# Hashed attention and a squared-ReLU layer: a table that shifts the order's priorities, and one more head in float32

## The chip, the cores and the metric

The kernel runs on one core of one Trainium2 chip. The metric is the device time of one execution in microseconds (us); lower is better. The core has a matrix engine (TensorE, PE; its weight loads are shown apart as PEld), a vector engine (VectorE, DVE), a scalar engine (ScalarE, ACT), a general engine (GpSimd, POOL) and a queue engine for DMAs (SyncE, SP). Each runs its own instructions strictly in the order in which the program lists them, and waits at an instruction until what it needs is there.

## The reference

Attention over 4 batches, 8 heads, 768 positions and 64 values per position, in which a query sees only keys of its own hash bucket (6 bits, the signs of six projections):

```
q_bits = (q @ proj > 0);  k_bits = (k @ proj > 0)
mask   = q_bucket[:, None] == k_bucket[None, :]
scores = where(mask, 0.125 * q @ k.T, -1e9)
attn   = exp(scores - max(scores));  attn = attn / (sum(attn) + 1e-9)
x      = attn @ v                       # reshaped to 3072 tokens x 512
h      = x @ w_in                       # 512 -> 2048
out    = (s * max(h, 0)**2 + b) @ w_out # 2048 -> 512
```

## The kernel before

A *slot* is 256 queries of one head of one batch: 96 slots, three to a head, in the order of the batches. For a slot PE multiplies queries and keys into three PSUM banks (L569 or L571, "lead"), DVE takes the row maximum (L577) and finishes it over a transpose that PE makes (L588, L592, then L590 and L599), PE adds the maximum's row and the low parts to the scores ("closing" matmuls, L609 or L611), ACT takes the exponentials (L616, three pieces of 512 columns), and PE multiplies them with the values (L639, or L641 and L642). The product goes through a division (L681 to L684) and a store to memory (`xd`, L686).

There are two forms. In a *plain* head (batch 0) the exponentials stay float32 and PE multiplies them in one float32 matmul (L639), with the sum of exponentials as ones beside the values. In the other heads each piece is split into a high part (ACT, L634) and a low part (POOL, L635), which PE multiplies in two matmuls (L641, L642), and the sum comes from DVE (L661) and two short matmuls (L669). Four heads of batch 0 have exact scores in float32 (buffers `eqa`, `eqb`); the others have split scores, whose hash rows are moved into place by DMAs on SP's queue (L458 to L461, L489 to L492; the last of them is `aq<-nat`). Exponentials of plain slots go around nine buffers, three to a slot.

The weights come as 64-bit words and are decoded to float32 high and low parts by ACT, DVE and POOL (L363 to L375, 32 times) during the first slots. From slot 23 on the expert layer can run: for 256 tokens PE multiplies with `w_in` (L718), ACT squares (L723 to L725), POOL makes the low part (L726), and PE multiplies with `w_out` (L735).

What sets the order: the program first records every step with its engine, a cost, what it reads and writes, and a priority `pr` (10 per slot, 1e5 and more for expert matmuls, 1e4 for the rest of the expert layer). `Plan.order` (L73) then plays the steps through: at each turn the engine that can start first takes, of its ready steps, the one of the lowest priority (L112 to L117). The result is written out engine by engine. So a priority does not move a step past what it depends on, but decides which ready step goes first; expert matmuls fill what is left.

Of the kernel before, what the change touches and what calls it, by code (L numbers as in the profile page):

```python
# [10 lines left out]
F32 = mybir.dt.float32  # L11
# [20 lines left out]
class Plan:  # L32
# [39 lines left out]

    def order(self):  # L73
        n = len(self.steps)
        left = [len(s[5]) for s in self.steps]
        users = [[] for _ in range(n)]
        for i, s in enumerate(self.steps):
            for d in s[5]:
                users[d].append(i)
        ready, other = [0.0] * n, [-9.0] * n  # L80
        free = {}
        moved = 0.0
        used = {}
        holder, todo, until, again, soon = {}, dict(self.size), {}, {}, []

        def clear(i, e):
            b = self.half.get(i)
            t = max([t for (n, o), t in used.items() if n == b and o != e], default=-9.0)
            if i in self.lock and self.lock[i][0] not in holder:
                t = max(t, again.get(self.lock[i][0], -9.0))  # L90
            return t

        def may(i):
            if i not in self.lock:
                return True
            b, g = self.lock[i]
            return holder.get(b, g) == g and (b != 4 or g in soon or g in holder.values() or all(self.steps[i][3] + BEHIND <= self.steps[j][3] for j in soon))
        open_ = {}
        for i in range(n):
            if not left[i]:  # L100
                open_.setdefault(self.steps[i][0], []).append(i)
        out = []
        while len(out) < n:
            best = None
            for e, every in open_.items():
                lst = [i for i in every if may(i)]
                if lst:
                    t = max(free.get(e, 0.0), min(max(ready[i], clear(i, e)) for i in lst))
                    if best is None or t < best[0]:
                        best = (t, e)  # L110
            t, e = best
            rank = lambda i: (self.steps[i][3], i)  # L112
            at = {i: max(ready[i], clear(i, e)) for i in open_[e] if may(i)}
            safe = [i for i in at if at[i] <= t and max(other[i], clear(i, e)) + self.soft.get(i, CHAIN) <= t] if e == PE else []
            i = min(safe, key=rank) if safe else min((i for i in at if at[i] <= t), key=rank)
            if not safe:
                i = min((j for j in at if at[j] <= t + LOOK.get(e, 0.0) * self.steps[i][1] and rank(j) <= rank(i)), key=rank)  # L117
            open_[e].remove(i)
            eng, cost, fn, pr, lag, deps = self.steps[i]
            start = max(free.get(e, 0.0), at[i])  # L120
            free[e] = start + cost
            end = start + cost + HOP[e]
            if e == SP:
                moved = max(moved, start + cost) + lag
                end += moved - start - cost
            else:
                end += lag
            out.append((start, i))
            if i in self.soon:
                soon.append(self.soon[i])  # L130
            if i in self.lock:
                b, g = self.lock[i]
                holder[b] = g
                todo[g] -= 1
                until[b] = max(until.get(b, -9.0), end)
                if not todo[g]:
                    again[b] = until[b]
                    if g in soon:
                        soon.remove(g)
                    del holder[b]  # L140
            if i in self.half:
                used[self.half[i], e] = end
            for u in users[i]:
                ready[u] = max(ready[u], end - (SAME[e] if self.steps[u][0] == e else 0.0))
                if self.steps[u][0] != e:
                    other[u] = max(other[u], end)
                left[u] -= 1
                if not left[u]:
                    open_.setdefault(self.steps[u][0], []).append(u)
        self.length = max(free.values())  # L150
        self.start = {i: t for t, i in out}
        return [i for _, i in sorted(out)]
# [5 lines left out]
CHAIN = 0.05  # L158
OFF = 0.4
BEHIND = 8.0  # L160
TURN = 1
LOOK = {DVE: 0.5, ACT: 0.0, POOL: 0.0}


# [1 line left out]
def lsh_attention_moe(ctx: ExitStack, tc, q, k, v, proj, w_in, w_out, s, b, out):  # L166
    nc = tc.nc
    B, H, S, D = q.shape
    DM, DF = w_in.shape
    P = 128  # L170
# [16 lines left out]
    wk = ctx.enter_context(tc.tile_pool(name="wk", bufs=1))  # L187
# [4 lines left out]
    bank = ps.tile([P, 8, 512], F32, name="bank")  # L192
# [5 lines left out]
    def tile_(name, shape, dt=F32):  # L198
        return const.tile(shape, dt, name=name)
# [44 lines left out]
    MX = tile_("mx", [P, CH])  # L244
# [11 lines left out]
    osb = tile_("osb", [P, 2, DM])  # L256
    misc = tile_("misc", [P, 8])
    thr, big, s_sb, b_sb, qk_sb = [misc[:, x:x + 1] for x in range(5)]


    ident = tile_("ident", [P, P])
    make_identity(nc, ident)

    for _ in range(10):
        nc.tensor.matmul(bank[:, 7, 0:P], ident, ident, start=True, stop=True)


    for x in SETS:
# [9 lines left out]
    for i in range(2):  # L278
        rows = slice(i * 64, (i + 1) * 64)
        for r in range(2):  # L280
            c = at[i] + r * NBITS
# [22 lines left out]
    for ks in KS:  # L304
        nc.vector.tensor_copy(ks[0:NR, 1], ones[0:NR].broadcast_to([NR, S]))
    nc.vector.tensor_copy(oner, ones.broadcast_to([P, P]))
    nc.vector.memset(MX, 0.0)
    for y in range(2):
        nc.vector.tensor_copy(zhl[:, y], MX)
    for x, y in ((s, s_sb), (b, b_sb)):  # L310
# [4 lines left out]
    visits, slots = [], []  # L315
# [22 lines left out]
            dec.append((w_out_w[f * P:(f + 1) * P, :], ("wo", f)))  # L338
    ND = len(dec)

    def decode(u, pr):
        src, key = dec[u]
        box = {}

        def new():
            box["t"] = wk.tile([P, 512, 2], I32, tag=f"w{u}", name=f"raw{u}")

        def swap():
            wt[key] = wk.tile([P, 2, 512], F32R, tag=f"w{u}", name=f"w{u}")

        def raw():
            return box["t"]
        rk, wk_ = [("raw", u)], [key + (0,), key + (1,)]
        g, gk = osb[:, u % 2, :], ("os", u % 2)
        gi = g.bitcast(I32)

        held = []
        if u >= NB:
            z = SETS[(u - NB) // 3]
            held = ([("vs", z, 0), ("vs", z, 1)], AK(z), KK(z))[(u - NB) % 3]  # L360
        plan.add(None, 0.0, new, [], rk + held, pr - 5)
        plan.add(ACT, 0.1, lambda: nc.scalar.dma_start(raw(), src.rearrange("p (n t) -> p n t", t=2)), KK("a") if u < PACE else [], rk + [("pace", u % PACE)], pr - 5, 5.0)
        act(512, lambda: nc.scalar.activation(g, raw()[:, :, 1].bitcast(F32), AF.Copy, scale=float(2.0**-112)), rk + [("pace", u % PACE)], [gk], pr, 0.06)  # L363
        act(512, lambda: nc.scalar.activation(raw()[:, :, 0], raw()[:, :, 0].bitcast(U32), AF.Copy, scale=float(2.0**-29)), rk, rk, pr, 0.06)
        dve(256, lambda: nc.vector.tensor_scalar(raw()[:, :, 1], gi, -2**31, None, ALU.bitwise_and), [gk], rk, pr, 0.6)
        dve(512, lambda: nc.vector.scalar_tensor_tensor(gi, gi, 3, raw()[:, :, 1], ALU.logical_shift_left, ALU.bitwise_or), rk, [gk], pr, 0.92)
        pool(512, lambda: nc.gpsimd.tensor_tensor(gi, gi, raw()[:, :, 0], ALU.add), rk, [gk], pr)  # L367
        plan.add(None, 0.0, swap, [], rk + wk_, pr)
        act(512, lambda: nc.scalar.copy(wt[key][:, 0], g), [gk], [key + (0,)], pr)
        if key[0] == "wo":  # L370
            if key[1] == 0:
                pool(512, lambda: nc.gpsimd.tensor_copy(bcs, g), [gk], ["bcs"], pr + 5)
            else:
                pool(512, lambda: nc.gpsimd.tensor_tensor(bcs, bcs, g, ALU.add), [gk], ["bcs"], pr + 5)
        pool(512, lambda: nc.gpsimd.tensor_tensor(wt[key][:, 1], g, f32(wt[key][:, 0]), ALU.subtract), [gk, key + (0,)], [key + (1,)], pr)  # L375
# [17 lines left out]
    def KK(x, r=(0, 1, 2, 3, 4)):  # L393
        return [("ks", x, i) for i in r]
# [107 lines left out]
    def prep_values(w, pr):  # L502
        bb, h = visits[w]["bb"], visits[w]["h"]
        x = visits[w]["x"]
        vk = [("vs", x, 0), ("vs", x, 1)]
        vd = v[bb, h].rearrange("(p t) d -> p t d", t=NT)
        if not bb:
            if x not in SETS:
                def new():
                    EV[x] = wk.tile([P, NT, 2, D], F32, tag=f"vs{x}", name=f"vs{w}")  # L510
# [22 lines left out]
        mean(bb, h, pr)  # L533

    def plain(i):
        return not slots[i][0]

    def et(z):
        return E[z] if z < NE else HL[z - NE]
# [15 lines left out]
    def scores(i, pr):  # L555

        bb, h, c, w = slots[i]
        x, y = visits[w]["x"], i % 2
# [5 lines left out]
        for p in range(NP_):  # L564
# [5 lines left out]
                        continue  # L570
                    nc.tensor.matmul(o, ks[0:HR + NR, 0, kt], aq[0:HR + NR, cs], start=m == 0, stop=m == 1, skip_group_check=True)  # L571
            pe(mmc(CH, 8 if exact else 2), lead, AK(x) + KK(x) if exact else AK(x, g=CG[c])  + KK(x, (0, 2, 4)), [("b", pb[p])], pr, True)
        turn = slots[i][0] >= TURN
        t, tk, nm, nk = MX, "mx", nmt[:, turn], ("nm", turn)

        sc = bank[:, b0:b0 + NP_].rearrange("p b (m n) -> p n b m", n=CH)
# [189 lines left out]
    for i in range(NSL):  # L766
        pr = 10.0 * i
        bb, h, c, w = slots[i]
# [46 lines left out]
MP = 1e4  # L815
PP = 0


# [1 line left out]
_INS = ['q', 'k', 'v', 'proj', 'moe_w_in', 'moe_w_out', 'moe_s', 'moe_b']  # L820
_OUTS = [((3072, 512), 'float32')]
# [21 lines left out]
```

## Time and profile before

| | us |
|---|---|
| median of 3 runs (1036.47, 1041.07, 1041.07) | 1041.07 |
| the profiled execution | 1038.18 |
| its span, first to last instruction | 1036.4 |
| PE busy | 999.8 (96%) |
| DVE, ACT, POOL busy | 685.2, 673.6, 654.5 |

Busy times are of the span. PE and the others work side by side; only the time in which PE does not work can be gained without taking work from it. A PE record is drawn from its start to a modelled end and overlaps the next one. A float32 matmul is two records.

### The profile page before, as it was taken

The page shows a single profiled execution, that of the slowest core. Times are in us where ns is not written, and L with a number is a line of the kernel's source. Part 1 is how long each engine was busy: PE and PEld are TensorE (multiplying, and loading weights), DVE is VectorE, ACT ScalarE, POOL GpSimd, SP SyncE. Part 2 cuts the span into 40 slices and gives each one's busy share as a digit, 9 for nine tenths or more (in the row PEclk, how much of TensorE's full clock was granted, in tenths as well). Part 3 has the DMA queues.
Part 4 walks back from the last instruction along what each step waited for, and adds up shares of the span by engine and source line. Part 5 has one row for each costly group of instructions (what it writes and reads, how often), then busy time and mean ns, then how long its engine had stood idle before and what let it go on. Part 6 is the DMA issues. An engine that isn't in the chain of part 4 may idle for free.

```text
span 1036.4 us, 18211 instructions
## 1 busy us (share of the span) xinstructions
PE 999.8 (96%) x6662; PEld 898.0 (87%) x6662; DVE 685.2 (66%) x893; ACT 673.6 (65%) x1325; POOL 654.5 (63%) x596
## 2 busy tenths in 40 slices
PE   8989889889999999999999999999999999999998
PEld 6867767769899999999999988999999999899997
DVE  5778787876787787778787778877787876100000
ACT  4767776677676777777777767776777677333322
POOL 2566775697777776777777667767767776312221
PEclk9999999999999999999999999999999999999999
DMA  7565764522422332333432332332432220201000
GB/s 180 145 171 137 195 180 124 151 57 58 111 71 73 99 94 58 108 89 78 108 91 62 93 99 58 88 105 66 109 99 68 73 66 11 82 1 61 31 22 20
DMA packets 93681, 93.07 MB, mean 90 GB/s; under 512 B 62744, under 2 KB 66328, under 8 KB 93592
## 3 DMA queue, kind: packets, MB, share of 16 engines
q1 hardware_dynamic: 88392, 74.87, 27.3%
q10 hardware_dynamic: 5200, 17.05, 5.6%
q8 instruction: 52, 0.85, 0.3%
q14 instruction: 37, 0.30, 0.1%
HBM read 48.24 MB, written 18.87 MB: 65 GB/s over the span
## 4 chain that ended last, share of the span: by engine, by line
PE 86%; POOL 4%; DMA 3%; DVE 2%; ACT 2%; issue 2%; SPq 0%; DVEq 0%; ACTq 0%; POOLq 0%
PE bank L718 26%; PE bank L735 25%; PE bank L571 5%; PE bank L611 5%; PE bank L642 5%; PE bank L641 5%; PE bank L639 4%; PE bank L569 2%; PE bank L669 2%; PE bank L451 2%; DMA aq<-nat 1%; POOL hl L635 1%; POOL osb L367 1%; DMA xd<-xsb 1%; PE bank L592 1%
## 5 line engine op out<-in xcount | busy, mean ns | idle before, releaser
L635 POOL TENSOR_TENSOR hl<-et,hl 128x512 fp32r<-128x512 f32 x216 | 279.6, 1321 | 119.9 <-ACT hl L634 100.6
L718 PE MATMUL bank<-xc,w 128*128 128x256 f32 x2304 | 337.5, 285 | 0.6 <-ACT rb L723 0.4
L718 PEld LDWEIGHTS bank<-xc,w 128*128 128x128 f32 x2304 | 305.4, 190 | 8.5 <-ACT rb L723 1.5
L735 PE MATMUL bank<-w,ghb 128*128 128x512 f32 x768 | 255.4, 399 | 0.0
L726 POOL TENSOR_TENSOR glb<-rb,ghb 128x512 fp32r<-128x512 f32 x96 | 125.0, 1302 | 120.4 <-ACT ghb L725 110.8
L577 DVE TENSOR_REDUCE mx<-bank 128x256 f32<-128x1536 f32 x96 | 168.1, 1751 | 5.1 <-PE bank L569 1.9
L661 DVE TENSOR_REDUCE zb<-et 128x256 f32<-128x1536 f32 x72 | 126.2, 1752 | 59.7 <-ACT et L616 56.7
L735 PE MATMUL bank<-w,glb 128*128 128x512 f32 x384 | 152.3, 398 | 0.7 <-POOL glb L726 0.7
L735 PEld LDWEIGHTS bank<-w,ghb 128*128 128x128 f32 x768 | 135.2, 189 | 18.1 <-issue 0.2
L616 ACT ACTIVATE et<-bank 128x512 f32<-128x512 f32 x240 | 132.6, 625 | 20.5 <-PE bank L611 12.1
L723 ACT ACTIVATE rb<-bank 128x512 f32<-128x512 f32 x96 | 57.5, 599 | 130.3 <-PE bank L718 127.3
L634 ACT CAST hl<-et 128x512 fp32r<-128x512 f32 x216 | 130.7, 664 | 0.4
L642 PE MATMUL bank<-hl,vs 128*128 128x256 f32 x432 | 113.7, 284 | 5.3 <-POOL hl L635 5.3
L641 PE MATMUL bank<-hl,vs 128*128 128x256 f32 x432 | 113.9, 284 | 0.0
L674 ACT ACTIVATE xpb<-bank,vmn 64x256 f32<-64x256 f32 x96 | 45.0, 469 | 96.6 <-PE bank L642 95.8
L571 PE MATMUL bank<-aq,ks 84*128 84x256 f32 x504 | 104.3, 294 | 3.4 <-DMA aq<-nat 3.0
L642 PEld LDWEIGHTS bank<-hl,vs 128*128 128x128 f32 x432 | 81.7, 189 | 13.7 <-POOL hl L635 7.8
L571 PEld LDWEIGHTS bank<-aq,ks 84*128 84x128 f32 x504 | 81.1, 190 | 10.6 <-issue 2.9
L681 DVE RECIPROCAL zpb<-zpb 128x256 f32<-128x256 f32 x48 | 83.6, 1741 | 5.7 <-ACT zpb L672 5.6
L641 PEld LDWEIGHTS bank<-hl,vs 128*128 128x128 f32 x432 | 81.7, 189 | 6.1
L743 DVE SCALAR_TENSOR_TENSOR osb<-bank,misc,bcs 128x512 f32<-128x512 f32 x22 | 16.2, 745 | 100.8 <-PE bank L735 100.7
L735 PEld LDWEIGHTS bank<-w,glb 128*128 128x128 f32 x384 | 72.2, 188 | 11.8 <-POOL glb L726 1.1
(121 smaller groups left out, 1565.0 us busy)
## 6 DMA issues: line engine op xcount, KB each, us to landing
xd<-xsb SPq DMA_DIRECT2D x48, 256.0 KB
xc<-xd SPq DMA_DIRECT2D x48, 256.0 KB
raw<-in_moe_w_in_dram ACTq DMA_DIRECT2D x16, 512.0 KB
raw<-in_moe_w_out_dram ACTq DMA_DIRECT2D x16, 512.0 KB
nat<-in_q_dram SPq DMA_DIRECT2D x32, 192.0 KB
nat<-in_k_dram SPq DMA_DIRECT2D x32, 192.0 KB
out_dram<-osb SPq DMA_DIRECT2D x22, 256.0 KB
ks<-aq SPq DMA_DIRECT2D x28, 192.0 KB
```

What stands on the lines that cost most here:

```text
L571: nc.tensor.matmul(o, ks[0:HR + NR, 0, kt], aq[0:HR + NR, cs], start=m == 0, stop=m == 1, skip_group_check=True)
L577: dve(S * TPC, lambda: nc.vector.tensor_reduce(t, sc, AX.XY, ALU.max), [("b", b) for b in pb], [tk], pr, 1.75)
L616: act(512, lambda p=p, z=z: nc.scalar.activation(et(z) if plain(i) else pairs(z), bank[:, pb[p]] if plain(i) else bank[:, pb[p]].rearrange ...
L634: act(512, lambda z=z, y=y: nc.scalar.copy(HL[2 * y].rearrange("p (m n) -> p m n", n=CH), pairs(z)), [("e", z)], [("hl", 2 * y)], pr, 0.05)
L635: pool(512, lambda z=z, y=y: nc.gpsimd.tensor_tensor(HL[2 * y + 1].rearrange("p (m n) -> p m n", n=CH), pairs(z), f32(HL[2 * y]).rearrange ...
L641: nc.tensor.matmul(av, VS[x][:, kt], HL[2 * y][:, ms], start=(kt == 0), stop=False)
L642: nc.tensor.matmul(av, VS[x][:, kt], HL[2 * y + 1][:, ms], start=False, stop=(kt == NT - 1))
L661: dve(S * TPC, lambda: nc.vector.tensor_reduce(ZB, es, AX.XY, ALU.add), [("e", z) for z in range(NE)], ["zb"], pr, 1.75)
L681: dve(CH, lambda: nc.vector.reciprocal(zp, zp), [], zk, pr + 20, 1.75)
L718: nc.tensor.matmul(hp, wt[("wi", n, cc)][:, m % 2, fs], xc[:, m // 2, :], start=(cc == 0 and m == 0), stop=(cc == NC_ - 1 and m == 2))
L726: pool(2 * CH, lambda r=r, gh=gh, gl=gl: nc.gpsimd.tensor_tensor(gl, r, f32(gh), ALU.subtract), [rk, hk], [lk], MP)
L735: nc.tensor.matmul(bank[:, 6 + t, :], (gh, gh, gl)[n][:, ts], wt[("wo", f)][:, n % 2], start=(f == 0 and n == 0), stop=(f == NF - 1 and n ...
```

## The change

Three things. The priorities that `order` compares are the old ones plus an offset from a table, `NUDGE`: it is looked up by the place of the step in the code (75 places, counted by line) and by the part of the run (five, cut at the priorities 30, 200, 330 and 820; everything of the expert layer is in the last). The offsets lie between -60 and 60, six slots' worth, and were found by random search. Then `NPL = 9` makes the first nine heads plain, where it was the eight of batch 0; `TURN = 8` counts heads where `TURN = 1` counted batches and chooses the same ones, and `NG = 0` adds no buffer. Last, the 10 matmuls at the start that have no use but to keep PE at work become 13 and read a zeroed tile in place of the identity.

```diff
     def order(self):
         n = len(self.steps)
+        sites = sorted({s[2].__code__.co_firstlineno for s in self.steps})
+        pr = []
+        for s in self.steps:
+            part = len(CUTS) if s[3] >= MP / 2 else sum(s[3] >= c for c in CUTS)
+            pr.append(s[3] + NUDGE.get(sites.index(s[2].__code__.co_firstlineno), {}).get(part, 0.0))
...
-            rank = lambda i: (self.steps[i][3], i)
+            rank = lambda i: (pr[i], i)
...
-TURN = 1
+TURN = 8
+NPL = 9
+NG = 0
...
+    nc.vector.memset(MX, 0.0)
+    for _ in range(13):
+        nc.tensor.matmul(bank[:, 7, 0:P], MX[:, 0:P], MX[:, 0:P], start=True, stop=True)
...
-    for _ in range(10):
-        nc.tensor.matmul(bank[:, 7, 0:P], ident, ident, start=True, stop=True)
...
-        if not bb:
+        if w < NPL:
...
     def plain(i):
-        return not slots[i][0]
+        return slots[i][3] < NPL
...
-        turn = slots[i][0] >= TURN
+        turn = slots[i][3] >= TURN
...
+CUTS = (30, 200, 330, 820)
+NUDGE = {
...
+    49: {0: 10.4, 1: 31.4, 2: -17, 3: 60, 4: -14},
...
+    52: {0: 60, 1: 58.7, 2: 40.4, 3: -25.7, 4: -60},
...
+}
```

Entry 49 is the exponentials, 52 the value matmuls. Lines of the changed kernel stand 10 further down than those of before in the functions below L343 (L639 is L649), and 7 in `dma` (L203 is L210).

TensorE, in slots 2 to 5 of the first batch. L609 and L619 close the scores of a slot, L639 and L649 are the value matmuls; `et` and `ex0` to `ex5` are the buffers of exponentials (slot 4 writes `ex0` to `ex2`, slot 2 `ex3` to `ex5`). Before:

```order
L569 MATMUL bank_64<-eqb_78,ekb_80 128x256 x2
L609 MATMUL bank_64<-zhl_90,oner_94 128x256 x6
L451 MATMUL bank_64<-ident_102,nat1_67 128x128 x3
L639 MATMUL bank_64<-ex0_82,evb_76 128x256 x2
L571 MATMUL bank_64<-aq0_68,ks0_72 128x256 x2
L639 MATMUL bank_64<-ex1_83,evb_76 128x256 x2
L639 MATMUL bank_64<-ex2_84,evb_76 128x256 x2
```

After:

```order
L602 MATMUL bank_64<-ident_116,nmt_93 8x128
L649 MATMUL bank_64<-ex4_86,eva_75 128x256 x2
L619 MATMUL bank_64<-zhl_90,oner_94 128x256 x6
L461 MATMUL bank_64<-ident_116,nat1_67 128x128 x3
L649 MATMUL bank_64<-ex5_87,eva_75 128x256
L581 MATMUL bank_64<-aq0_68,ks0_72 128x256 x2
L649 MATMUL bank_64<-ex5_87,eva_75 128x256
L581 MATMUL bank_64<-aq0_68,ks0_72 128x256 x4
L598 MATMUL bank_64<-ident_116,mx_88 128x128 x2
L602 MATMUL bank_64<-ident_116,nmt_93 8x128
L649 MATMUL bank_64<-et_81,evb_76 128x256 x2
```

Before, the closing matmuls of slot 4 are followed, after three transposes, by slot 4's own values; after, they are followed by the values of slots 2 and 3.

SP's queue, at the hash rows of the sixth head (`aq0`, `ks0`, `nat1`); `xd` is a stored result, which waits for POOL's `xsb`. Before:

```order
L203 DMA xd0_1_1_156<-xsb_96 128x512
L203 DMA aq0_68<-bq0_70 8x768
L203 DMA bq0_70<-aq0_68 64x768
L203 DMA ks0_72<-nat1_67 12x768
L203 DMA xd0_1_2_157<-xsb_96 128x512
L203 DMA aq0_68<-nat1_67 12x768
```

After:

```order
L210 DMA xd0_1_1_159<-xsb_96 128x512
L210 DMA ks0_72<-nat1_67 12x768
L210 DMA aq0_68<-nat1_67 12x768
L419 DMA nat1_67<-in_q_dram 128x6x64
L419 DMA nat1_67<-in_k_dram 128x6x64
L210 DMA xd0_1_2_160<-xsb_96 128x512
```

The second store moves from ahead of the last hash row to behind it and behind two loads.

POOL, at the end of the weights (L367, L374, L375 decode them; L635 is the low part of a piece, L726 of the expert layer). Before:

```order
L635 TENSOR_TENSOR hl5_1602<-et_81,hl4_1593 128x512
L663 TENSOR_TENSOR zhl_90<-zb_89,zhl_90 128x256
L726 TENSOR_TENSOR glb_99<-rb_97,ghb_98 128x512
L367 TENSOR_TENSOR osb_100<-osb_100,raw29_1603 128x512
L374 TENSOR_TENSOR bcs_65<-bcs_65,osb_100 128x512
L375 TENSOR_TENSOR w29_1737<-osb_100,w29_1737 128x512
L367 TENSOR_TENSOR osb_100<-osb_100,raw30_1522 128x512
L635 TENSOR_TENSOR hl1_1534<-et_81,hl0_1530 128x512
L375 TENSOR_TENSOR w30_1775<-osb_100,w30_1775 128x512
```

After:

```order
L736 TENSOR_TENSOR glb_99<-rb_97,ghb_98 128x512
L377 TENSOR_TENSOR osb_100<-osb_100,raw31_1464 128x512
L384 TENSOR_TENSOR bcs_65<-bcs_65,osb_100 128x512
L385 TENSOR_TENSOR w31_1832<-osb_100,w31_1832 128x512
L736 TENSOR_TENSOR glb_99<-rb_97,ghb_98 128x512
L539 TENSOR_TENSOR vs10_1849<-vn_74,vs10_1849 128x6x64
L645 TENSOR_TENSOR hl1_1760<-et_81,hl0_1754 128x512
L645 TENSOR_TENSOR hl3_1834<-et_81,hl2_1767 128x512
```

Before, low parts stand between the last weights; after, the last weight stands ahead of the first low part.

## Rows read from the trace of the kernel before

**Rows 1.** The page's busy line: busy us, share of the span, instructions.

```profile
PE 999.8 (96%) x6662; PEld 898.0 (87%) x6662; DVE 685.2 (66%) x893; ACT 673.6 (65%) x1325; POOL 654.5 (63%) x596
```

**Rows 2.** Busy time by stretch: the columns stand in the first line.

```profile
core 0: us, PE busy (x) PEld busy (x) DVE busy (x) ACT busy (x) POOL busy (x), PEclk, DMA share, GB/s
0.00:225.00 225.00, 195.72 (x1130) 162.66 (x1130) 170.99 (x243) 151.49 (x299) 143.30 (x130) 0.99 0.57 152
225.00:920.00 695.00, 691.29 (x4827) 633.81 (x4828) 509.56 (x643) 485.07 (x966) 485.40 (x447) 1.00 0.30 80
...
175.00:200.00 25.00, 22.36 (x127) 19.33 (x126) 20.28 (x26) 16.42 (x35) 12.03 (x13) 0.93 0.50 134
200.00:225.00 25.00, 19.90 (x134) 17.07 (x133) 19.52 (x26) 17.95 (x34) 24.81 (x20) 1.00 0.32 83
```

**Rows 3.** The chain of waits, 60 to 226 us: start, length, what.

```profile
69.12 1.03 POOL xsb L684
...
71.90 3.82 DMA aq<-nat
...
186.15 1.65 DVE zpb L681
...
194.23 1.07 PE bank L718 x9
...
199.89 2.52 POOL hl L635 x2
...
214.09 1.28 POOL osb L367
```

**Rows 4.** Groups by line: busy us, mean ns | idle before.

```profile
L718 PE MATMUL bank<-xc,w 128*128 128x256 f32 x2304 | 337.5, 285 | 0.6 <-ACT rb L723 0.4
...
L616 ACT ACTIVATE ex<-bank 128x512 f32<-128x512 f32 x48 | 25.3, 594 | 2.3 <-PE bank L609 1.5 <-PE bank L611 0.8
...
L681 DVE RECIPROCAL zpb<-zpb 128x256 f32<-128x256 f32 x48 | 83.6, 1741 | 5.7 <-ACT zpb L672 5.6
```

**Rows 5.** The chain of waits, longest pieces: matmuls in a row.

```profile
2.16 4.64 PE bank L265 x20
...
52.77 1.73 PE bank L639 x8
...
411.40 2.16 PE bank L718 x18
```

**Rows 6.** Whom PE waited for, 0 to 226 us: total, times, longest.

```profile
PE bank L642 <- POOL hl L635: 3.7, 4, 1.8
PE bank L639 <- ACT ex L616: 3.6, 7, 1.0
PE bank L571 <- DMA aq<-nat: 3.0, 3, 1.2
PE bank L451 <- DVE zhl L599: 2.8, 3, 1.6
PE bank L592 <- DVE nmt L590: 2.7, 5, 1.0
PE bank L265 <- POOL ident masks.py:199: 2.2, 1, 2.2
...
PE bank L639 <- ACT et L616: 1.2, 2, 0.9
```

**Rows 7.** Groups by line, page: the steps a plain head lacks.

```profile
L635 POOL TENSOR_TENSOR hl<-et,hl 128x512 fp32r<-128x512 f32 x216 | 279.6, 1321 | 119.9 <-ACT hl L634 100.6
...
L634 ACT CAST hl<-et 128x512 fp32r<-128x512 f32 x216 | 130.7, 664 | 0.4
```

**Rows 8.** DVE in order of time, 0 to 10 us: start, length.

```profile
0.89 0.38 DVE L269 MEMSET eva<- 128x384 f32 x1 [0.89 <-PEq L828]
...
2.40 0.27 DVE L307 MEMSET mx<- 128x256 f32 x1
```

**Rows 9.** SP's queue, waits of 0 to 226 us: total, times, longest.

```profile
SPq L513 <- PE bank L639: 7.8, 1, 7.8
```

More of the change, by code (lines that the diff above doesn't have):

```diff
@@ L96, in may @@
             b, g = self.lock[i]
-            return holder.get(b, g) == g and (b != 4 or g in soon or g in holder.values() or all(self.steps[i][3] + BEHIND <= self.steps[j][3] for j in soon))
+            return holder.get(b, g) == g and (b != 4 or g in soon or g in holder.values() or all(pr[i] + BEHIND <= pr[j] for j in soon))
         open_ = {}
@@ L118, in order @@
             open_[e].remove(i)
-            eng, cost, fn, pr, lag, deps = self.steps[i]
+            eng, cost, fn, _, lag, deps = self.steps[i]
             start = max(free.get(e, 0.0), at[i])
@@ L306, in lsh_attention_moe @@
     nc.vector.tensor_copy(oner, ones.broadcast_to([P, P]))
-    nc.vector.memset(MX, 0.0)
     for y in range(2):
@@ L339, in lsh_attention_moe @@
     ND = len(dec)
+    G = [(osb[:, x], ("os", x)) for x in range(2)] + [(wk.tile([P, 512], F32, tag=f"xc{x}", name=f"g{x}"), ("xc", x)) for x in range(NG)]
     def decode(u, pr):
@@ L353, in decode @@
         rk, wk_ = [("raw", u)], [key + (0,), key + (1,)]
-        g, gk = osb[:, u % 2, :], ("os", u % 2)
+        g, gk = G[u % len(G)]
         gi = g.bitcast(I32)
```

73 rows, old and new, of the table NUDGE are left out of this document.

## The prediction

> **What bounds the kernel now.** I read the page first, then the busy time by stretches, then TensorE's waits and the chain of waits in the stretch that differs from the rest. The page shows TensorE (PE) 96% busy and every other engine near 65% [rows 1]: the time is PE's work plus PE's idle time. The stretches say where the idle time is. From 225 to 920 us, the end of the attention work, PE is idle for 3.7 us of 695. In the first 225 us it is idle for 225 - 195.7 = 29.3 us, while the vector engine (DVE) is busy for 171.0, ScalarE (ACT) for 151.5 and GpSimd (POOL) for 143.3 [rows 2]. None of them is full there; the work of one slot (256 queries of one head) goes PE - DVE - PE - DVE - PE - ACT - PE, and PE has nothing else until the first expert matmuls (L718), which in the chain begin at 194.23 us [rows 3].
>
> The busy share hides some of it. A 256-column matmul is drawn 285 ns long [rows 4], but 18 of them in a row take 2.16 us, 120 ns each [rows 5]: each gap is about 0.165 us longer than it looks. With some 45 waits in the stretch that is 7 us, so the idle time there is nearer 37 us.
>
> By the Trainium skill ("Trainium Kernel Development and Optimization", Performance Expectations) a matmul's busy share is a bad measure, and the share of the weight loads a good one. The trace bears this out: weight loads are 162.7 / 225 = 72% busy early and 633.8 / 695 = 91% later, by which the early stretch would hold 225 - 162.7 / 0.91 = 46 us to win and not 29 to 37. By that share the case in which all early idle time goes would end near 1038 - 46 + 3 = 995 us. I take that as too much, as float32 matmuls, which stand mostly early, take longer per weight load.
>
> Who ends PE's waits in that stretch [rows 6]: the low halves of POOL (L642, 3.7 us), the exponentials of ACT (L639, 3.6 and 1.2), a DMA that carries hash rows (L571, 3.0), the identity at the start (2.2). The other 15.6 us are mostly DVE's short steps of the row maximum (L590, L599), each under 3 us in total.
>
> **The change part by part.** Of the constants only `NPL` = 9 does something: head 0 of batch 1, the ninth, becomes plain float32 in its values. The table has an entry for each of the 75 places, and the rows of the new order above show that it moves steps on every engine.
>
> *One more head in float32.* It adds 18 matmuls. One is two records, and eight records take 1.73 us, so 0.432 us each [rows 5]: +7.8. It removes 36 at 0.120 (-4.3) and six of the sum of exponentials (-0.7). PE does 2.8 us more, and as PE is full after 225 us all of it counts. Off PE it removes 9 splits of POOL at 1.32 us and 9 casts of ACT at 0.66 [rows 7]. Where PE is full that is worth nothing, but POOL is 24.8 us busy in the 25 us up to 225, and PE is idle there for 5.1 [rows 2]: the last weight splits (L367, L374, L375) and the first slots' low halves (L635) fall together. In the chain POOL stands from 199.89 us on and still at 214.09 [rows 3]. In the new order the last weight split stands ahead of the first low half, so this collision goes. I count the whole wait on low halves, -3.7.
>
> *Values behind the exponentials.* A plain slot's values wait for an exponential (0.59 us, [rows 4]) and ACT's queue before it. I counted what stands in PE's order between the first closing score matmuls of a slot (L609, L611) and its first value matmul (L639), priced at the spacings above. Over the first 24 slots the median goes from 0.9 us to 2.4, and in the first seven slots from 0.5 to 1.9 up to 4.2 to 9.5. So 4.0 of the 4.8 us go.
>
> *The hash rows.* The chain shows the pattern at 69.12 us: POOL's low half of a stored result, then the store on SP's queue, then `aq<-nat` behind it in the same queue (3.82 us), then L571 [rows 3]. In the new order two of the stores stand behind `aq<-nat`. But a value load into a buffer that late values hold (L513) stands ahead of it. I count 2.0 of 3.0.
>
> *DVE's short steps.* The order gives them little directly: DVE work that stands between a slot's row maximum and its last row step sums to 45.7 us over 24 slots before and to 48.0 now. What helps is that PE has more beside it: from the last score matmul to the transposes of the maximum (L588) 3.9 us on average before, 6.0 now. A bad case stands in the chain at 186.15 us: a reciprocal, 1.74 us long, runs ahead of a short row step [rows 3, 4]. Between 0 and all of 15.6 I take a third, 5.0, as the DVE order itself stays as crowded.
>
> *Hidden parts.* About 24 gaps gone at 0.165: -4.0. The granted clock is 0.93 of full speed from 175 to 200 us, the only such stretch of the early part [rows 2], so PE was at the lower of its two levels (1.2 GHz) for about 3.5 us; this follows the idle time before it and costs up to 1.75. I count -1.0.
>
> *The start.* 13 warm-up matmuls in place of 10 take 26 records x 0.232 = 6.0 us instead of 20, 4.64 [rows 5]. They now wait for the memset of `MX`, which as DVE's first step could end at 0.89 + 0.27, near 1.2 us [rows 8], where the identity came at 2.16. With the hop the warm-up ends about 0.5 us later: +0.5.
>
> *After 225 us.* The table moves every step there too. I compared the same distances in slots 24 to 95: closing scores to the low-half matmul 7.4 us (median) before and 7.8 now, its least 5.1 and 6.6. Expert matmuls fill between. I cost it at nothing; the cover is that filler, and if it failed each slot could lose about 1 us.
>
> Sum: -3.7 - 4.0 - 2.0 - 5.0 - 4.0 - 1.0 + 2.8 + 0.5 = -16.4 us. The profiled execution took 1038.18 us (span 1036.4 and 1.8 around it), so 1021.8; it lies 2.9 below the median 1041.07 of the runs, whose least is 1036.47; as the runs spread over 4.6 us, I don't shift it. I forecast 1022.
>
> **The rivals.**
> *All of the early idle time goes.* For it: no engine is full in the stretch. Against it: DVE is at 171 of 225 us, and its queue is in order. Everything but the start: -27.1 of visible gaps and -7.4 hidden, +3.3 for the head and the start: 1007.0.
> *The waits only change place.* Values later on PE hold the nine buffers of exponentials, three slots' worth, for longer, so that ACT waits for PE and the scores for ACT. For it: the DVE steps, the largest group, are no freer in their queue. Then only POOL's collision goes: 3.7 + 0.7 - 3.3, about 1037.1.
> *SP's queue stalls, and it is slower.* Before, the queue waited once for values ahead of a value load, 7.8 us [rows 9]. With values later, each of the five split-score heads of the stretch (2, 3, 5, 6 and 8) can meet this wait with its hash rows queued behind the load, and PE then has no scores to begin. At 7.8 each that is 39 us against the gain: 1022 + 39 = 1061; with three of five 1046. It decides from three heads on. Against it: between a head's second hash and its first scores PE now has 12, 6, 7 and 5 us of work (heads 2, 3, 5 and 6) where it had 8, 7, 5 and 4.
>
> **How the numbers follow.** Forecast 0.62, with a range of its own from 1012 (3.7, 4.8 and 3.0 of the named waits, 10.4 of the DVE group, 7 hidden and 1 of the clock, less the 3.3 added) to 1034 (nothing of the DVE group, half of the other gains); all idle time gone 0.15; change of place 0.12; SP's stall 0.11. Half a percent of 1041, 5 us, is about what can be told from no change, so the first two are faster (0.77), the third is no change (0.12) and the fourth slower (0.11). From 1004 to 1041 leaves out the slower case and the lowest part of the second.
>
> **What would show it.** In the first 225 us PE's idle time falls from 29.3 to about 15 us, the first expert matmul begins some 15 us before 194, no wait on low halves is among the first of the stretch, exponentials cost PE under 1 us there, and POOL is below 23 of 25 us wherever one looks. After that stretch idle stays under 5 us. I am wrong if PE's idle time early stays above 25 us, if it waits for `aq<-nat` more than before, or if new waits stand after 225 us.

## The result and the profile after

The changed kernel takes 1024.78 us (median of 4 runs, 1022.44 to 1026.69) against 1041.07 (4 runs, 1036.47 to 1041.2): a ratio of 0.9844, 95% interval 0.9818 to 0.987, faster by 1.6%. The forecast was 1022. The profiled execution took 1026.69 us, 11.5 less than that of before (1038.18); the section on reasons shows why the medians stand further apart.

Busy time by stretch after the change, with the columns of [rows 2]:

```profile
core 0: us, PE busy (x) PEld busy (x) DVE busy (x) ACT busy (x) POOL busy (x), PEclk, DMA share, GB/s
0.00:225.00 225.00, 205.00 (x1168) 169.54 (x1169) 166.72 (x239) 148.46 (x292) 135.71 (x122) 0.98 0.56 152
225.00:920.00 695.00, 694.85 (x4872) 641.60 (x4872) 506.13 (x640) 489.26 (x967) 482.94 (x444) 1.00 0.29 80
175.00:200.00 25.00, 22.95 (x142) 19.43 (x143) 19.32 (x28) 17.36 (x36) 15.14 (x13) 1.00 0.77 198
200.00:225.00 25.00, 25.00 (x159) 22.05 (x159) 18.16 (x25) 18.18 (x37) 21.86 (x18) 1.00 0.33 84
```

PE's idle time in the first 225 us falls from 29.3 to 20.0 us (the prediction said about 15), and after that from 3.7 to 0.15. The last row is the clearest: in the stretch where POOL was full, PE now has no idle time and POOL has some.

Whom PE waited for, 0 to 226 us (total, times, longest), where [rows 6] stood before:

```profile
PE bank L581 <- DMA aq<-nat: 2.6, 1, 2.6
PE bank L621 <- DVE bq L609: 2.2, 3, 1.2
PE bank L649 <- ACT zpb L682: 1.5, 2, 1.0
PE bank L602 <- DVE nmt L600: 1.3, 4, 0.5
...
PE bank L581 <- ACT ex L626: 1.3, 3, 0.5
...
PE bank L270 <- DVE mx L268: 1.2, 1, 1.2
...
PE bank L579 <- ACT et L626: 1.0, 2, 0.5
...
PE bank L579 <- ACT ex L626: 0.5, 1, 0.5
...
PE bank L649 <- ACT xpb L684: 0.4, 1, 0.4
```

The wait on low halves (3.7 us before) is gone, and so are the waits of the value matmuls (L639, now L649) for exponentials (4.8). But ACT appears again on other lines: scores (L579, L581) wait for its exponentials to finish reading a bank, 1.3 + 1.0 + 0.5 us, and value matmuls wait for it to read the product before theirs (L682, L684), 1.5 + 0.4. That is 4.7 us, about what was there. What ACT's exponentials (L626) wait for in the same stretch:

```profile
ACT ex L626 <- PE bank L619: 8.0, 7, 3.8
ACT et L626 <- PE bank L621: 5.1, 4, 3.0
ACT ex L626 <- PE bank L621: 4.4, 4, 2.5
```

That is 17.5 us of waits for closing matmuls, where it was 6.1 before (L616 for L609 and L611); no wait of theirs in the view is for late values to free a buffer. All waits of PE in the view together go from 29.1 us in 44 to 19.3 in 30: POOL's low halves -3.7, DVE -3.6 (12.4 to 8.8 without the start), the start -1.0 (the longer warm-up takes it back: the first transpose runs at 6.75 us, 6.59 before), DMA -0.4, ACT -1.1.

Some 3.5 us of the gain lie behind 225 us, where [rows 2] left 3.7 idle. POOL's last decode step runs at 220.8 us and its first low half at 227.9; before, the first low half ran at 197.9 and the last decode steps (L374) at 219.8, so both kinds of work shared the queue for over 20 us. By 250 us PE has done 144 expert matmuls (L728), where it had done 120 of them (L718). The attention itself is no faster in this pair: the transpose of the row maximum (L602, L592 before) of slot 24 runs at 197.3 us (194.0 before), of slot 93 at 854.9 (854.4), with 3.4 us more of the clock lost on the way (last section). What is gained is expert work done beside it between about 195 and 260 us.

By the Trainium skill ("Trainium Kernel Development and Optimization", Performance Expectations) the share of weight loads tells more than PE's busy share. In the early stretch it rose from 162.7 to 169.5 of 225 us, in the rest to 641.6 of 695. The trace doesn't settle it: the two gains, 6.9 and 7.8 us, sum to 14.7, those of busy time, 9.3 and 3.6, to 12.9; the spans of this pair differ by 11.5 us, runs at an equal clock by 14.5 (below). Nor is the prediction's 91% a mark for every stretch: from 200 to 225 us, with PE busy throughout, the share is 22.05 of 25, 88%.

### The profile page after: what moved, and what is told of

It reads as the page before. It is cut to its first block, busy times and chain, and to the rows that moved or that the text cites. A ratio compares the mean times of both kernels' runs of the same rounds, so it can differ in the third digit from the quotient of the medians.

```text
span 1024.9 us, 18271 instructions
## 1 busy us (share of the span) xinstructions
PE 1001.2 (98%) x6672; PEld 902.2 (88%) x6672; DVE 677.5 (66%) x886; ACT 670.9 (65%) x1312; POOL 641.9 (63%) x584
## 4 chain that ended last, share of the span: by engine, by line
PE 94%; DVE 2%; ACT 1%; issue 1%; DMA 1%; POOL 0%; SPq 0%; DVEq 0%; POOLq 0%; ACTq 0%
PE bank L728 27%; PE bank L745 26%; PE bank L581 6%; PE bank L649 6%; PE bank L621 6%; PE bank L651 5%; PE bank L652 5%; PE bank L579 3%; PE bank L461 2%; PE bank L679 2%; PE bank L602 1%; PE bank L490 1%; PE bank L491 1%; PE bank L492 1%; PE bank L527 1%
## 5 line engine op out<-in xcount | busy, mean ns | idle before, releaser
L645 POOL TENSOR_TENSOR hl<-et,hl 128x512 fp32r<-128x512 f32 x207 | 267.6, 1322 | 125.6 <-ACT hl L644 102.4
L728 PE MATMUL bank<-xc,w 128*128 128x256 f32 x2304 | 327.7, 284 | 0.9 <-ACT rb L733 0.9
L728 PEld LDWEIGHTS bank<-xc,w 128*128 128x128 f32 x2304 | 301.9, 191 | 7.8 <-ACT rb L733 1.3
L745 PE MATMUL bank<-w,ghb 128*128 128x512 f32 x768 | 258.3, 399 | 0.0
L626 ACT ACTIVATE et<-bank 128x512 f32<-128x512 f32 x234 | 130.7, 623 | 23.0 <-PE bank L621 12.8
L671 DVE TENSOR_REDUCE zb<-et 128x256 f32<-128x1536 f32 x69 | 120.8, 1751 | 31.4 <-ACT et L626 27.6
L644 ACT CAST hl<-et 128x512 fp32r<-128x512 f32 x207 | 128.1, 663 | 0.4
L581 PE MATMUL bank<-aq,ks 84*128 84x256 f32 x504 | 108.2, 299 | 4.0 <-DMA aq<-nat 2.6
L651 PE MATMUL bank<-hl,vs 128*128 128x256 f32 x414 | 108.2, 283 | 0.0
L652 PE MATMUL bank<-hl,vs 128*128 128x256 f32 x414 | 107.5, 281 | 0.0
L684 ACT ACTIVATE xpb<-bank,vmn 64x256 f32<-64x256 f32 x96 | 45.0, 469 | 76.6 <-PE bank L652 55.8
L581 PEld LDWEIGHTS bank<-aq,ks 84*128 84x128 f32 x504 | 81.3, 190 | 12.1 <-ACT ex L626 5.6
L651 PEld LDWEIGHTS bank<-hl,vs 128*128 128x128 f32 x414 | 78.1, 189 | 7.5
L652 PEld LDWEIGHTS bank<-hl,vs 128*128 128x128 f32 x414 | 78.1, 189 | 7.0
L621 PE MATMUL bank<-bq,ks 128*128 128x256 f32 x504 | 76.2, 286 | 2.3 <-DVE bq L609 2.2
```

The costliest lines, as they stand in the source:

```text
L621: nc.tensor.matmul(o, ks[:, 1, kt], bq[:, cs], start=False, stop=m == 1, skip_group_check=True)
L626: act(512, lambda p=p, z=z: nc.scalar.activation(et(z) if plain(i) else pairs(z), bank[:, pb[p]] if plain(i) else bank[:, pb[p]].rearrange ...
L644: act(512, lambda z=z, y=y: nc.scalar.copy(HL[2 * y].rearrange("p (m n) -> p m n", n=CH), pairs(z)), [("e", z)], [("hl", 2 * y)], pr, 0.05)
L645: pool(512, lambda z=z, y=y: nc.gpsimd.tensor_tensor(HL[2 * y + 1].rearrange("p (m n) -> p m n", n=CH), pairs(z), f32(HL[2 * y]).rearrange ...
L651: nc.tensor.matmul(av, VS[x][:, kt], HL[2 * y][:, ms], start=(kt == 0), stop=False)
L652: nc.tensor.matmul(av, VS[x][:, kt], HL[2 * y + 1][:, ms], start=False, stop=(kt == NT - 1))
```

## The experiments

Each kernel was timed against the one before on the same chip; the experiments ran on four chips, on which the kernel before took 1039.2 to 1040.6 us, so comparisons between experiments are good to about 1 us. Where "at clock 0.998" stands, only runs with that mean granted clock are compared (the last section shows why this is the sharper measure; before: 14 runs, 1035.9 to 1038.2, mean 1036.9). A kernel that loses more of the clock by its own waits is flattered by it, so the medians stand beside it. Parts of the table are 0 to 4, by its cuts; part 2 ends at slot 32.

**The head alone.** The new warm-up stays in.

```diff
+NUDGE = {}
```

> All offsets of the table are zero; the ninth head in float32 and the new warm-up stay. Theory A (the prediction): most of the gain is in slots 0 to 20, where values now stand behind later work, so the head alone gives only the end of the collision on POOL, 3.7 us of waits, less 3.3 us added: no change, 1037 to 1041 us. Theory B (the two traces): both kernels reach slot 24 and slot 93 at the same time within 3.5 us, and what differs is PE idle between 200 and 260 us, where POOL had weights and low halves at once; the head alone then gives most of the 16 us: 1026 to 1032 us, idle of PE from 200 to 225 us below 1.5 us (5.1 before).

Measured: 1035.04 us (12 runs), ratio 0.9945 [0.992, 0.9969]; at clock 0.998 three runs of 1029.5 to 1031.2, so -6.7 (-4.8 between the medians). That lies between the ranges of the two theories. Its waits, 0 to 226 us, then its busy PE by stretch (busy, records, granted clock, DMA share, GB/s):

```profile
PE bank L649 <- ACT ex L626: 3.8, 7, 1.2
PE bank L581 <- DMA aq<-nat: 3.5, 3, 1.4
...
PE bank L602 <- DVE nmt L600: 2.7, 5, 1.0
PE bank L649 <- ACT et L626: 1.7, 2, 0.9
```

```profile
200.00:225.00 25.00, 24.06 (x157) 1.00 0.39 98
200.00:260.00 60.00, 58.50 (x390) 1.00 0.28 72
260.00:900.00 640.00, 638.50 (x4486) 1.00 0.31 84
```

The main waits but POOL's stand much as before (compare [rows 6]), and the idle time from 200 to 225 us falls from 5.1 to 0.94 us. The first low half now runs at 229.5 us, behind the last decode step at 219.4: the head alone ends the collision, without the new order. The first expert matmul, though, runs at 198.8 us, later than before, and by 250 us 120 are done, as before: the earlier and denser expert work comes with the table. So one head more in float32 is worth more than the -0.4 of the sum (-3.7 + 2.8, and 0.5 for the warm-up).

**The table alone.**

```diff
-NPL = 9
+NPL = 8
```

> The whole table, but eight plain heads as before; in the order of POOL seven low halves stand among the last weights again, as before. Theory A: the gain of the early order stays, less the 3.7 us of POOL and with 2.8 us less work: 1024 to 1028 us. Theory B: the collision is back, 1035 to 1041 us, with 4 us or more of PE idle between 200 and 250 us.

Measured: 1050.67 us (6 runs), ratio 1.0103 [1.0079, 1.0127]: slower, outside the ranges of both theories. One stretch shows where, PE alone:

```profile
175.00:200.00 25.00, 17.52 (x77) 0.79 0.64 156
```

7.5 us of idle and a clock of 0.79, just before the first expert matmuls; from 200 to 260 us another 5.7. POOL's kinds of work are mixed again: the first low half runs at 210.7 us, the last decode step at 232.7. That the table, with the ninth head split, puts steps ahead of others that PE needs sooner is my reading; no run isolates it.

**Parts 0 and 1; parts 2 to 4; parts 0 to 2.** All with nine plain heads.

```diff
+NUDGE = {k: {p: x for p, x in d.items() if p < 2} for k, d in NUDGE.items()}
```

> The offsets of slots 0 to 19 alone (parts 0 and 1), with the ninth head. Values stand 4 to 9 us of PE work behind their scores in the first seven slots, as in the changed kernel. Theory A: close to the whole change, 1024 to 1029 us. Theory B: as with the head alone, within 3 us of it, 1026 to 1033 us; PE idle from 0 to 200 us as without the table, near 24 us.

```diff
+NUDGE = {k: {p: x for p, x in d.items() if p >= 2} for k, d in NUDGE.items()}
```

> The offsets from slot 20 on alone (parts 2, 3 and 4), with the ninth head. Theory A: the early gain is missing, 1035 to 1040 us. Theory B: the head's gain and whatever the order after slot 20 adds to it: 1022 to 1029 us.

```diff
+NUDGE = {k: {p: x for p, x in d.items() if p < 3} for k, d in NUDGE.items()}
```

> The offsets up to slot 32 alone (parts 0, 1 and 2), with the ninth head; attention after slot 32 and the expert layer stand as before. The prediction costs the table after 225 us at nothing: the same as the whole change, 1023 to 1027 us, PE idle from 260 to 900 us at most 2 us. A rival, that the late offsets keep the expert matmuls fed: slower than the whole change by 3 us or more, with idle after 260 us as in the head alone (1.5 us) or above.

Measured: parts 0 and 1, 1035.38 us (0.9958 [0.9941, 0.9976]); parts 2 to 4, 1052.73 (1.0113 [1.0085, 1.0141]); parts 0 to 2, 1022.28 (0.9831 [0.9802, 0.9859]). From 175 to 200 us PE is busy for 19.00 us at clock 0.86, for 19.23 at 0.73 and for 22.95 at 1.00. The first two halves are no better than the head alone, or 18 us worse, and the second misses the ranges of both theories; together with part 2 the early parts give everything. Offsets beyond slot 32 are worth nothing that can be measured. That the fault of the halves lies in the seam between parts 1 and 2 is argued from the stretch in which it shows; no run isolates it. Parts 0 to 2 are also the best version run, level with the whole change.

**Only the exponentials and the values.** Entries 49 and 52, parts 0 to 2.

```diff
+NUDGE = {k: {p: x for p, x in d.items() if p < 3} for k, d in NUDGE.items() if k in (49, 52)}
```

> Of the table only the rows of the exponentials and of the value matmuls, up to slot 32, with the ninth head: values stand 3 to 8 us of PE work behind their scores in the first seven slots, and nothing else is moved on purpose. Theory A (the prediction): the waits of values on exponentials (5.5 us in the head alone) go and 4 us or more come with them, 1026 to 1031 us against 1035 for the head alone. Theory C: they change place, to scores that wait for ACT to free their banks and to values that wait for ACT to free bank 3 (4.9 us together in the whole change); no gain, 1032 to 1038 us.

Measured: 1033.69 us (12 runs), 0.9948 [0.9925, 0.9971]; at clock 0.998, 1031.1 to 1032.7 (4 runs): no better than the head alone. Its waits, 0 to 226 us, in a profiled execution that was its slowest (1041.35, clock 0.990):

```profile
PE bank L581 <- DMA aq<-nat: 3.7, 2, 2.3
PE bank L581 <- DMA ks<-nat: 1.9, 1, 1.9
PE bank L579 <- ACT et L626: 1.9, 1, 1.9
...
PE bank L581 <- ACT ex L626: 1.3, 3, 0.7
PE bank L649 <- ACT xpb L684: 1.3, 2, 0.8
PE bank L649 <- ACT ex L626: 1.2, 2, 0.9
```

The values' wait for exponentials fell from 3.8 + 1.7 to 1.2, as the prediction meant; in its place stand the scores' waits for ACT (3.2), the product's reader (1.3) and hash rows (5.6, was 3.5).

**The rest of the table without these two.**

```diff
+NUDGE = {k: {p: x for p, x in d.items() if k not in (49, 52) or p > 2} for k, d in NUDGE.items()}
```

> The whole table but the rows of the exponentials and values up to slot 32, which are zero; the ninth head stays. Values stand 0.5 to 2.5 us behind their scores, as in the kernel before. Theory A: the rest of the table keeps its gains, 1027 to 1031 us. Theory C: the offsets only work together; without two of them the order stalls as with half the table, 1033 us or more, with a lower granted clock between 150 and 225 us.

Measured: 1108.21 us (6 runs), 1.0657 [1.0619, 1.0694]. Its waits, 0 to 226 us:

```profile
PE bank L602 <- DVE nmt L600: 12.5, 19, 2.9
PE bank L621 <- DVE bq L609: 9.1, 12, 1.9
PE bank L619 <- DVE zhl L609: 4.7, 6, 2.0
```

26 us of waits for DVE's short steps. The 73 us over the head alone are about half idle time and half clock: up to 920 us PE idles for 59.7 us against 26.2, and the mean clock of 0.963 against 0.993 is some 34 us of the span. I read it so: the late values are what PE does while DVE finishes a row maximum, and the other offsets take away what stood there before. The run before fits that (with these two rows alone, all waits for DVE sum to 8.7 us, against 11.4 in the head alone, the start left out), but no run takes exponentials and values apart. So the offsets can't be priced one by one: the two alone are worth nothing, the rest without them costs 73 us over the head alone, together they gain.

**The old warm-up.** The whole change with the 10 matmuls on the identity.

```diff
-    for _ in range(13):
-        nc.tensor.matmul(bank[:, 7, 0:P], MX[:, 0:P], MX[:, 0:P], start=True, stop=True)
...
+    for _ in range(10):
+        nc.tensor.matmul(bank[:, 7, 0:P], ident, ident, start=True, stop=True)
```

> The whole change but the warm-up, which is 10 matmuls on the identity as before. The prediction prices the new one at +0.5 us: 1023 to 1026 us here, no change that can be told. A rival, that the longer warm-up keeps TensorE's clock up in the first 30 us: slower than the whole change by 2 us or more, with a granted clock below 0.97 in the first 50 us.

Measured: 1025.13 us (6 runs), 0.9857 [0.9823, 0.9891]. No difference that can be told in time. In the traces the first transpose runs at 5.96 us with the old warm-up and at 6.75 with the new: +0.8 there, where +0.5 was said.

**A second head in float32, no table.**

```diff
-NPL = 9
+NPL = 10
...
+NUDGE = {}
```

> The head alone (no offsets) with one more head: ten plain heads. The prediction prices a plain head at +2.8 us of PE work where nothing waits. The collision on POOL is gone already with nine, so theory B expects the tenth to cost that and no more: 1036 to 1040 us at the median, 2 to 4 us above the head alone (1035; 1030 at a granted clock of 0.998), and 1032 to 1034 at 0.998. A rival, that every plain head relieves the queues of ACT, DVE and POOL and so gains: 1028 to 1033 us at the median.

Measured: 1034.75 us (11 runs), 0.9943 [0.9925, 0.9962]; at clock 0.998, 1030.1 to 1030.6 (3 runs): the same as one head. PE by stretch:

```profile
200.00:260.00 60.00, 59.48 (x382) 1.00 0.30 77
260.00:900.00 640.00, 639.72 (x4489) 1.00 0.31 82
```

The median lies between the two ranges; the 2.8 us of added work don't appear. Against one head the idle time of these stretches falls from 3.0 to 0.8 us, which pays most of it.

**Hash rows first.** Parts 0 to 2, and on SP's queue the two short rows ahead of the two long ones, for each split head.

```diff
+        queue = keep + [blk[1], blk[2], blk[0], blk[3]] + queue[last + 1:]
```

> As the parts 0 to 2 (1022.3 us), with one edit: of the four DMAs that end a split head's preparation, the two hash rows (ks<-nat, aq<-nat) go ahead of aq<-bq and bq<-aq on SP's queue. The prediction counted 2 of 3 us on the hash rows; the trace shows 2.6 still there at 134 us, where aq<-nat stands behind two DMAs that wait for earlier ones to land. If the queue is the cause, that wait falls below 1 us and the time by 1 to 3 us: 1019 to 1022. If the landing of aq<-bq is needed just as late, no change, 1021 to 1024, and PE waits for aq<-bq instead. A rival: the queue now stands at aq<-nat and holds up the loads of the next head: slower, 1025 or more.

Measured: 1026.3 us (6 runs), 0.9861 [0.9836, 0.9885]; at clock 0.998 one run of 1022.01 (parts 0 to 2: 1021.2 to 1022.3) and at 0.999 one of 1023.53. No gain. The median lies in the rival's range, but the loads of the next head go out no later (134.58 us, 135.50 in parts 0 to 2), so the stall that it names isn't there; the other four runs had clocks of 0.994 to 0.996. To see why, first the chain of waits of the whole change around its longest wait (start, length, what):

```profile
127.73 5.01 DMA ks<-bq
...
132.81 0.51 SPq L210
...
133.37 0.74 SPq L210
...
134.21 4.60 DMA aq<-nat
...
139.05 0.47 PE bank L581 x2
```

`aq<-nat` is the last of four copies that SP sends from 131.81 to 134.21 us, after it stood there for earlier copies of the head to land (`ks<-aq`, then `ks<-bq`), and takes 4.6 us itself. With the new queue the waits on PE are these (lines 3 further down: L584 is L581):

```profile
PE bank L584 <- ACT ex L629: 2.3, 3, 1.5
...
PE bank L584 <- DMA aq<-bq: 1.6, 2, 0.9
```

The wait for `aq<-nat` is gone, but another copy, and the exponential ahead of these scores, stand nearly as late.

**POOL crowded.** Parts 0 to 2, with nine subtractions of 128x512 on POOL that belong to no part of the computation, one ahead of each of the first nine low halves.

```diff
+            if i in extra:
+                nc.gpsimd.tensor_tensor(osb[:, 0], osb[:, 0], osb[:, 0], ALU.subtract)
```

> As the parts 0 to 2 (1022.3 us), with nine subtractions of no use on POOL (128x512, about 1.3 us each), one ahead of each of the first nine low halves, where in the kernel before nine steps of the weights stood among them. Theory B (POOL's collision cost what the ninth head gave back): PE waits for low halves again, 3 to 5 us with the idle time around it, 1026 to 1030 us. If expert matmuls cover it, 1021 to 1024.

Measured: 1029.37 us (6 runs), 0.9891 [0.9864, 0.9917]; at clock 0.998, 1025.6 to 1028.5 (3 runs), some 5.4 us above parts 0 to 2 alone. PE, 200 to 260 us (59.87 busy without the added work):

```profile
200.00:260.00 60.00, 57.80 (x361) 1.00 0.27 69
```

and in the waits of the whole run (L654 is L652):

```profile
PE bank L654 <- POOL hl L646: 2.0, 5, 0.6
```

Putting 9.4 us of POOL work (nine subtractions, 1.05 us each in the trace) back at this place brings back the low halves' wait and takes 5.4 us, of which the named wait shows only 2.0.

**A tenth head, with the table.** Parts 0 to 2.

```diff
-NPL = 9
+NPL = 10
```

> As the parts 0 to 2 (1022.3 us, PE idle 0.13 us from 200 us to 900), with a tenth plain head. PE has no idle time left after 200 us that a plain head could fill, so the price of +2.8 us should be seen whole: 1024 to 1027 us, about 1024.5 at a granted clock of 0.998. The rival is what two plain heads did without the table, where the tenth cost nothing at the median (1034.8 against 1035.0): 1021 to 1023. A second rival: its steps stand where the offsets of slot 20 to 32 were not made for them, and PE stalls near 200 us: 1030 or more.

Measured: 1043.23 us (12 runs), 1.0023 [1.0004, 1.0042]. The chain of waits:

```profile
184.45 0.52 SPq L210
...
185.02 4.27 DMA aq<-nat
...
189.54 1.62 PE bank L581 x6
```

and two waits of SP's queue, 0 to 226 us:

```profile
SPq L523 <- PE bank L649: 19.8, 2, 12.6
...
SPq L210 <- DMA ks<-aq: 11.2, 6, 5.3
```

PE waits 5.0 us for a hash row, and the clock of 175 to 200 us is 0.86. SP stands for 12.6 us, until 173.2, at a load of values that waits for value matmuls (L649), sends the head's first copies from 173.85, and stands for 5.3 us, until 182.1, for one of them to land; the last hash row goes out at 185.02. The wait for values is the one that the prediction's third rival named (7.9 us in the whole change); whether it is what makes the row late, no run isolates, as in parts 0 to 2, without the long wait, the same copies begin only 2 us earlier, at 171.89. Without the table a tenth head cost nothing; with it, 21 us against nine, of which 8.7 are drawn idle time up to 920 us and about 8 lie in the clock (0.989 for 0.997 in the profiled runs). Of eight, nine and ten plain heads the table gains only with nine.

## Why the prediction was right, and where not

Time and sign were right, the time in part by luck. The five gains of waits and gaps were counted at 18.7 us and the traces show some 10 of them; the clock went the other way; and 3.6 us came from behind 225 us, where nothing was counted. The forecast also stood on the profiled execution of before: against that of after the change is -11.5 us, not -16.4. Step by step:

- *Low halves, -3.7:* right in its place, and the part that the runs show best. But it was mis-sized: the head as a whole, with the new warm-up, is worth -6.7 at an equal clock, not -0.4. Part of the price was in waits of other names: from 200 to 260 us the head alone takes 3.9 us of idle time, and from 260 to 900 another 1.9. The crowded POOL shows the same in reverse. That the idle time after 225 us [rows 2] was a tail of the collision holds for 1.7 us at most, those up to 300 us; nearly all the rest stands after 600.
- *Values behind the exponentials, -4.0:* this step failed. The named wait went away as said, and 4.7 us came back where scores and products wait for ACT. The rival "the waits only change place" was right for this one term, though not by the path that it named: ACT's exponentials wait for closing matmuls (17.5 us), not for buffers that late values hold. I counted order positions on PE and left ACT's own queue out: ACT now waits longer for the closing matmuls, and the next scores wait until its exponentials have read their bank.
- *Hash rows, -2.0:* -0.4. The rival of a stalled SP queue did not come in this kernel: the queue waits 7.9 us for values ahead of a value load, 7.8 before. With a tenth head that wait grows to 19.8 us and PE waits for the same DMA.
- *DVE's short steps, -5.0:* -3.6. The cause named, more work for PE beside them, fits: without the late exponentials and values these waits grow to 26 us.
- *Hidden gaps, -4.0:* 14 waits fewer, not 24; at 0.165 that is -2.3.
- *The clock, -1.0:* wrong in sign in the profiled run. The stretch from 175 to 200 us rose from 0.93 to 1.00 as said, but two others fell. In the first 225 us before lost 1.7 us of clock and after 5.1; the last section has the rows. This is most of why the two profiled executions stand 11.5 us apart and runs at an equal clock 14.5 (1036.9 against 1022.4, one run of the whole change, and 1021.2 to 1022.3, three of parts 0 to 2); the 16.3 between the medians rests on four runs of either kernel.
- *The head's 2.8 us of PE work:* worked out from rows 5, but never seen in a run's time; with the second head, 2.2 us less idle time paid for most of it.
- *The first expert matmul 15 us earlier:* 4.4 us (189.56 for 193.99). Expert work came not much earlier but denser, up to 260 us.
- *After 225 us nothing:* right for the offsets beyond slot 32, wrong for the idle time there: 3.7 us before, 2.05 with the head alone, 0.15 with both.

So at an equal clock the head gives about -6.7 and the table, on top of it, about -8; drawn idle time up to 920 us goes the same way, from 33.0 us to 26.2 with the head alone and 20.2 with both. Which of its offsets bring the 8 is not settled: parts 0 to 2 together hold all of it, and each smaller piece run alone gave nothing or lost. Of the profiled run's sums, idle -12.8 and clock +3.4 make -9.4 of the span's -11.5; the other 2.1 us are in what the view doesn't draw as idle, near the -2.3 of the gaps.

## What to carry to other kernels

A searched table of order offsets need not survive an edit: here either half of it, or the table with one head more or less in the other form, lost 10 to 28 us against the whole change, so search again after an edit. Look for the place where the queues of two phases meet on one engine, as the last weights and the first low halves on POOL here: its price here was larger than the wait that bore its name. And before a gain is counted for a wait taken away, follow the engine that was waited for to its next step, and see who waits there.

## What the runs showed of the hardware

Runs of one kernel differ mostly by the granted clock. Of 73 runs of the kernel before on four occasions, the 14 at a mean clock of 0.998 took 1036.9 us on average, the 14 at 0.993 1041.1 and the four at 0.990 1043.7: some 0.85 us for each 0.001. A thousandth of the span is 1.04 us, so the lower clock accounts for most of a spread of 8 us; runs at 0.998 still spread over 2.3.

The profiled run of after shows two such losses. PE by stretch of 5 us:

```profile
20.00:25.00 5.00, 3.44 (x18) 0.87 0.68 232
25.00:30.00 5.00, 5.00 (x23) 0.50 0.67 187
30.00:35.00 5.00, 5.00 (x27) 0.95 0.00 0
...
135.00:140.00 5.00, 2.35 (x15) 0.97 0.33 99
140.00:145.00 5.00, 4.84 (x21) 0.69 0.74 197
```

Before, in the second of these places, and at its own one loss ahead of 225 us:

```profile
135.00:140.00 5.00, 3.58 (x20) 1.00 0.35 119
140.00:145.00 5.00, 3.55 (x30) 1.00 0.77 201
...
185.00:190.00 5.00, 2.36 (x12) 0.83 0.21 81
190.00:195.00 5.00, 5.00 (x25) 0.83 0.64 152
```

What is missing to 1.00, times 5 us, is the loss: 3.4 and 1.7 us after, 1.7 before. Where a clock of 0.50 stands, PE runs at the lower level, 1.2 GHz for 2.4, and does the same matmuls more slowly while it looks fully busy: two transposes (L598) that take 0.23 us at 20.23 us take 0.43 at 28.89. Each of the three losses follows idle time: 1.6 us idle in the row of the first, 2.65 (the wait for `aq<-nat`) in that of the second, 2.64 in that of before. Before, with as much idle time in all from 135 to 145 us as after, but spread (1.42 and 1.45), it kept its clock. These rows suggest that idle time moved together can cost clock that the same idle time spread out does not; no run here tests it. The table has fewer waits, and in this run lost 3.4 us more of the clock.
